# A convolution and two gated MLPs on one core: the head reordered, block 0's softmax first and block 1's moved to GpSimd

## The chip, the cores and the metric

The kernel runs on one core of a Trainium2 chip. Its time is the device time of one execution in microseconds; the median of the runs counts. The engines are TensorE (PE; its weight loads are shown as PEld), VectorE (DVE), ScalarE (ACT), GpSimd (POOL) and SyncE (SP), which only issues DMAs. A TensorE matmul writes PSUM; GpSimd reaches SBUF alone.

## The reference, cut to what matters

```python
# 2 x 4096 tokens of 192 features; 8 heads of 24 features, 7 taps
w = exp(weight_gen - max(weight_gen)); w = w / (sum(w) + 1e-9)      # over the 7 taps of a head
out[s, h] = sum_k w[s, h, k] * x_pad[s + k, h]                      # causal, 6 zero rows ahead
xn = out / sqrt(mean(out**2) + 1e-6) * rms_g
y = (silu(xn @ w_gate) * (xn @ w_val)) @ w_out                      # 192 -> 1536 -> 192
h = y @ w_in; z = (h * sigmoid(1.702 * h)) @ w_out2                 # 192 -> 2048 -> 192
```

All in float32. A matmul of the MLPs is made of three products of float32 halves (high by high, low by high, high by low), so each operand exists as a high and a low tile.

## The kernel before

The 8192 tokens lie on 128 partitions, 64 to each, and are worked off in 16 blocks of 4 columns (512 tokens). For a block, `conv_ops` makes the seven products with the softmax weights, their sum, the mean square (`sq`, ScalarE), its power -0.5 (`root`, GpSimd) and the scaled rows `xr`. `transpose_x` turns these to the four operands `xh`, `xl`, `xsh`, `xsl` (two transposed halves on TensorE; high part on ScalarE, low part on VectorE).

A *unit* is one step of the MLPs: `(1, b, m)` is block b's m-th of 12 up steps of the first MLP, `(2, b, i)` one of 8 of the second. `U1` issues its matmuls: 9 pairs (upper and lower half of the array run side by side) into `pg` and `pv`, then ScalarE's `silu` of `pg`; `second()` is VectorE's `p = p * pv` and ScalarE's copy `h`; `third()` is VectorE's `l = p - h`. `D1` is the unit's down product, 5 pairs, which go in with the matmuls of a later unit: `pend` holds them until unit i + 2. The list `units` is the order. Blocks 0 and 1 are interleaved, with block 0 `LAG` ahead: (1,0,0) (1,0,1) (1,1,0) (1,0,2) (1,1,1) (1,0,3) ... Before and after, unit 24 is (2,0,0), the first of the second MLP.

The engines work in the order in which the program issues (a manual schedule), so the place of a line in the main loop is its place in a queue.

The weights come as 64-bit words and are decoded *piece* by piece (`piece`), with three pieces in flight. A piece is `x1` on ScalarE, `x2`, `x2m` (masks) on VectorE; then `x3` (shift), `x4`, `x5` (low half) on VectorE; then `x6` (high half) on ScalarE. `x5` also loads the next piece by SP. `piece_steps` finishes the oldest piece in flight (`x6`), does `x3` to `x5` of the next and `x1` to `x2m` of the one behind it. `need` lists the pieces by the unit that first uses them, `run_work` forces them `LOOK` units ahead, and `some` spends each unit's credit (`room`), which is about one call of `piece_steps` in a unit.

The head stands ahead of the loop. Both blocks' softmaxes are made on VectorE (`softmax_ops`: maximum, subtraction, ScalarE's exponential, sum, 1e-9, reciprocal, product); block 0's weights lie in PSUM. Block 0's taps are VectorE's (14 products and 12 additions in PSUM), block 1's products GpSimd's, with TensorE summing them by a matmul with the identity (`ident`). Then squares and roots of both blocks, block 0's scaling and turn, and block 1's turn in unit 0.

The softmax of blocks 2 to 4 is started at unit `start_at`, that of (1, 1, 7); its exponential, between two table loads on ScalarE, stands one unit later. `Y` makes the second MLP's operands `yh`, `yl`, `ysh`, `ysl`.

Of the kernel before, what the change touches and what calls it, by code (L numbers as in the profile page):

```python
# [9 lines left out]
F32 = mybir.dt.float32  # L10
# [8 lines left out]
P = 128  # L19
# [11 lines left out]
BLOCKS = [4] * 16  # L31
GROUPS = [(0, 1), (1, 2), (2, 5), (5, 8), (8, 11), (11, 14), (14, 16)]
AHEAD = 4
LAG = 1
LAG2 = 3
NST = 3
LOOK = 1
# [5 lines left out]
def gated_conv_mlp(ctx: ExitStack, tc: tile.TileContext, xp, wg, w1, wo1, w2, wo2, g, out):  # L43
# [117 lines left out]
        nc.sync.dma_start(out=t, in_=wg[:, T0[b0] * 56:(T0[b0] + n) * 56])  # L161
        return t

    def softmax_ops(gi, t, dst=None):
# [5 lines left out]
        d = t if dst is None else dst  # L170
        d3 = d.rearrange("p (q k) -> p q k", k=TAPS)
        mx = smw.tile([P, G], F32, tag="mx", name=f"mx{gi}")
        step = 64
        parts = [(a, min(a + step, G)) for a in range(0, G, step)]
        pre, post = [], []
        for a, b in parts:
            def f(a=a, b=b):
                nc.vector.tensor_reduce(out=mx[:, a:b], in_=t3[:, a:b, :], axis=AX.X, op=ALU.max)

            def f2(a=a, b=b):  # L180
                nc.vector.tensor_tensor(
                    out=t3[:, a:b, :], in0=t3[:, a:b, :],
                    in1=mx[:, a:b].unsqueeze(2).to_broadcast([P, b - a, TAPS]), op=ALU.subtract)
            w = 7.5 * (b - a) + 70
            pre += [(w, f), (w, f2)]

        def ex():
            nc.scalar.activation(out=t, in_=t, func=AF.Exp)
        for a, b in parts:
            def f(a=a, b=b):  # L190
                nc.vector.tensor_reduce(out=mx[:, a:b], in_=t3[:, a:b, :], axis=AX.X, op=ALU.add)

            def f1(a=a, b=b):
                nc.vector.tensor_scalar_add(out=mx[:, a:b], in0=mx[:, a:b], scalar1=1e-9)
                nc.vector.reciprocal(out=mx[:, a:b], in_=mx[:, a:b])  # L195

            def f2(a=a, b=b):
                nc.vector.tensor_tensor(
                    out=d3[:, a:b, :], in0=t3[:, a:b, :],
                    in1=mx[:, a:b].unsqueeze(2).to_broadcast([P, b - a, TAPS]), op=ALU.mult)  # L200
            w = 7.5 * (b - a) + 70
            post += [(w, f), (4 * (b - a) + 150, f1), (w, f2)]
        for b in range(b0, b1):
            o = (T0[b] - T0[b0]) * 56
            wn_of[b] = d[:, o:o + BLOCKS[b] * 56].rearrange("p (q k) -> p q k", k=TAPS)
        return pre, ex, post

    def load_x(*bs):
        T = sum(BLOCKS[b] for b in bs)
        t0 = T0[bs[0]]  # L210
        t = big.tile([P, (T + HALO) * D], F32, tag="x", name=f"x{bs[0]}")
        cuts = [0] + [T0[b] + BLOCKS[b] + HALO - t0 for b in bs]
        for c0, c1 in zip(cuts, cuts[1:]):
            nc.sync.dma_start(out=t[:, c0 * D:c1 * D], in_=xp[:, (t0 + c0) * D:(t0 + c1) * D])
        for b in bs:
            xch[b] = t[:, (T0[b] - t0) * D:]

    def conv_ops(b):

# [14 lines left out]
        if b < 2:  # L234
            S = T // 2
            sums_of = [pacc.tile([P, NM], F32, tag=f"{n}{b}", name=f"{n}c_{b}") for n in "ab"]
            acc_of = [sums_of[j // S][:, (j % S) * D:(j % S + 1) * D] for j in range(T)]
        else:
            acc = att.tile([P, T, D], F32, tag="acc", name=f"acc{b}")
            acc_of = [acc[:, j] for j in range(T)]  # L240
        if b == 1:
            def tap(k):
                for i, ps in enumerate(sums_of):
                    tag = (("yh", "yl"), ("ysh", "ysl"), ("yh0", "yl0"))[k % 3][i]
                    pr = ytp.tile([P, NM], F32R, tag=tag, name=f"pr{k}_{i}").bitcast(F32)[:, :S * D]
                    mul(nc.gpsimd, k, pr, i * S, (i + 1) * S)
                    nc.tensor.matmul(ps[:, :S * D], ident, pr, start=k == 0, stop=k == TAPS - 1)
            ops += [(cost, lambda k=k: tap(k)) for k in range(TAPS)]
        elif b == 0:
            n = S * D  # L250

            def tap(k):
                for i, ps in enumerate(sums_of):
                    mul(nc.vector, k, prod[:, i * n:(i + 1) * n] if k else ps[:, :n], i * S, (i + 1) * S)
                for i, ps in enumerate(sums_of if k else ()):
                    nc.vector.tensor_tensor(out=ps[:, :n], in0=ps[:, :n], in1=prod[:, i * n:(i + 1) * n], op=ALU.add)  # L256
            ops += [(cost, lambda k=k: tap(k)) for k in range(TAPS)]
        else:
            total = acc.rearrange("p t d -> p (t d)")

# [9 lines left out]
        def sq():  # L270
            room = xr if b != 1 else ytp.tile([P, NM], F32R, tag="yh", name="sq1").bitcast(F32).unsqueeze(1)
            for j in range(T):
                nc.scalar.activation(out=room[:, j if b != 1 else 0, 0:D], in_=acc_of[j], func=AF.Square,
                                     accum_out=ss[:, j:j + 1])
        ops.append((1500, sq))

        def root():
            nc.gpsimd.tensor_scalar(out=ss, in0=ss, scalar1=1.0 / D, scalar2=1e-6,
                                    op0=ALU.mult, op1=ALU.add)
            nc.gpsimd.tensor_tensor(out=ri, in0=ss, in1=half[:, :T], op=ALU.pow)  # L280
        ops.append((500, root))

        def sc(j):
            nc.vector.tensor_scalar_mul(out=xr[:, j, 0:D], in0=acc_of[j], scalar1=ri[:, j:j + 1])
            if b >= TURN:
                return
            i = (j + T // 2) % T if b < 2 else j
            nc.scalar.mul(out=xr[:, i, D:2 * P], in_=acc_of[i][:, P:D], mul=ri[:, i:i + 1])
        for j in range(T):
            ops.append((230, lambda j=j: sc(j)))  # L290
        xrow[b] = xr
# [36 lines left out]
    def transpose_x(b, halves=False):  # L328
# [6 lines left out]
        l = xtp.tile([P, NM], F32R, tag="xl", name=f"xl{b}")  # L335
        sh = xtp.tile([P, NM], F32R, tag="xsh", name=f"xsh{b}")
        sl = xtp.tile([P, NM], F32R, tag="xsl", name=f"xsl{b}")
        pa, pb = sums(b, "x_")
        xT[b] = (h, l, sh, sl)
        if halves:  # L340

# [13 lines left out]
        def split(acts=True, dves=True):  # L355
            for c, ps, i in parts:
                h_, l_ = ((h, l), (sh, sl))[c]
                h_, l_ = h_[:, :N], l_[:, :N]
                if i is not None:
# [239 lines left out]

    units = []  # L600
    for m in range(M1):
        units += [(1, 0, t) for t in range(len([u for u in units if u[1] == 0]), min(M1, m + LAG + m // 3 + 1))]
        units += [(1, 1, m)]
    for t in range(PAIRS + LAG2):
        units += [(2, 0, t)] if t < PAIRS else []
# [111 lines left out]
    with ExitStack() as order:  # L717
# [11 lines left out]
        warm = sml.tile([P, TM], F32, tag="ri", name="warm")  # L729
        nc.scalar.activation(out=warm, in_=half, func=AF.Exp)  # L730
        wn0 = pu.tile([P, NM], F32, tag="u", name="wn0")
        pre, ex, post = softmax_ops(0, sm[0], wn0[:, 0:BLOCKS[0] * 56])
        pre1, ex1, post1 = softmax_ops(1, sm[1])
        run(pre)
# [1 line left out]
        run(pre1)  # L736
        ex1()
        run(post)
        run(post1)
        nc.scalar.activation(out=warm, in_=half, func=AF.Silu)  # L740
        conv, conv1 = conv_ops(0), conv_ops(1)
        run(conv[:TAPS])
        run(conv1[:TAPS])
        for r in line:
            r[0].pop(0)()
        for f in [c[TAPS + k][1] for c in (conv, conv1) for k in range(2)]:
            f()
        for f in line[0].pop(0) + line[0].pop(0) + line[1].pop(0):
            f()
        for f in line.popleft().pop(0):  # L750
            f()
        run(conv[TAPS + 2:])
        split = transpose_x(0)
        for f in line[0].pop(0):
            f()
        split()
        for f in line[0].pop(0):
            f()
        line[0].append([])
        run(conv1[TAPS + 2:])  # L760
# [8 lines left out]
        for i, u in enumerate(units):  # L769
# [67 lines left out]
            second, third = (U1 if kind == 1 else U2)(b, m, lambda *ups: matmuls(ups, downs, kind == 2 and b < 2))  # L837
            todo = [v / 2 for v in (room(i) if i < pos[1, 2, 0] else (share(0, i), share(1, i)))]
            if i == 0:
                split = transpose_x(1)  # L840
                split(dves=False)
                second()
                split(acts=False)
                third()
                some(todo)
                some(todo)
                for f in line[0].pop(0):
                    f()
            elif i < pos[1, 2, 0]:
                run(behind)  # L850
# [73 lines left out]
```

## Time and profile before

| | |
|---|---|
| runs | 1229.76 us median of 3 (1228.94 to 1229.93) |
| profiled execution | 1228.96 us |
| its span, first to last instruction | 1227.0 us |
| granted TensorE clock, mean | 0.998 |

The profile is of one execution. Times are microseconds from the span's start. An engine is busy while it executes an instruction; what it waits for stands in brackets behind the first instruction after the pause. Where short instructions overlap, the distance between two starts is what one costs its engine, and the duration what the next engine waits for. The granted clock is a share of 2.4 GHz.

### The profile page before, as it was taken

The numbers are of one execution on the slowest core, as the hardware profiler recorded it, in microseconds if no ns is written. First come the engines' busy times: TensorE is split into PE (matmuls) and PEld (weight loads), VectorE is DVE, ScalarE is ACT, GpSimd is POOL, SyncE is SP. The second block draws the span as 40 slices with busy tenths as digits, with TensorE's granted clock in tenths as the row PEclk, the third lists the DMA queues.
The fourth block names the chain that finished last, engine by engine and source line by source line (L and its number), as shares of the span: only waits on it lengthen the run. The fifth ranks groups of instructions, "written<-read, shape, count | busy, mean of one in ns | idle before, by whom it ended". The sixth has DMA issues, their size and how long they took to land.

```text
span 1227.0 us, 26917 instructions
## 1 busy us (share of the span) xinstructions
PE 1210.3 (99%) x10316; PEld 1114.1 (91%) x10316; DVE 774.3 (63%) x1300; ACT 651.0 (53%) x1275; POOL 32.1 (3%) x53
## 2 busy tenths in 40 slices
PE   6999999999999999999999999999999999999998
PEld 3888999988999999999999998999988888988897
DVE  8998967857465574755747567464665746545432
ACT  4667664644545455464545645445464544544553
POOL 4000000000000000000000000000000000000000
PEclk9999999999999999999999999999999999999999
DMA  6884311010111001100100011010110011000000
GB/s 203 255 253 148 116 57 47 1 41 24 33 43 34 13 20 34 30 33 17 60 6 26 34 31 34 10 31 33 31 33 13 20 34 31 1 16 17 1 14 13
DMA packets 35615, 58.03 MB, mean 47 GB/s; under 512 B 8288, under 2 KB 21344, under 8 KB 35488
## 3 DMA queue, kind: packets, MB, share of 16 engines
q1 hardware_dynamic: 35264, 56.13, 14.7%
q8 instruction: 81, 1.33, 0.5%
q14 instruction: 46, 0.38, 0.1%
q10 hardware_dynamic: 224, 0.20, 0.1%
HBM read 43.71 MB, written 6.29 MB: 41 GB/s over the span
## 4 chain that ended last, share of the span: by engine, by line
PE 96%; DVE 2%; ACT 1%; issue 0%; DMA 0%; POOL 0%; DVEq 0%; POOLq 0%; ACTq 0%
PE a L381 24%; PE ph L381 22%; PE pg L381 18%; PE b L381 17%; PE pv L381 15%; DVE xr L229 0%; DVE p L490 0%; DVE ac L256 0%; DVE bc L256 0%; DMA wraw<-in_wg 0%; PE ax L352 0%; POOL ri L280 0%; DVE l L494 0%; ACT h L491 0%; DVE mx L195 0%
## 5 line engine op out<-in xcount | busy, mean ns | idle before, releaser
L381 PE MATMUL a<-h,o 64*128 64x512 f32 x1788 | 517.4, 391 | 0.0
L381 PEld LDWEIGHTS a<-h,o 64*128 64x128 f32 x1788 | 328.5, 184 | 13.7
L514 DVE TENSOR_TENSOR l<-p,h 128x512 fp32r<-128x512 f32 x256 | 176.1, 691 | 242.5 <-ACT p L508 241.1
L381 PE MATMUL b<-h,o 64*128 64x512 f32 x896 | 310.8, 392 | 0.0
L381 PE MATMUL b<-l,o 64*128 64x512 f32 x896 | 310.4, 392 | 0.0
L381 PE MATMUL a<-l,o 64*128 64x512 f32 x894 | 309.3, 391 | 0.0
L507 ACT ACTIVATE h<-ph 128x512 fp32r<-128x512 f32 x256 | 153.7, 600 | 204.2 <-PE ph L381 198.2
L381 PE MATMUL pv<-xh,w 64*128 64x512 f32 x768 | 240.8, 393 | 0.2
L381 PE MATMUL pg<-xh,w 64*128 64x512 f32 x768 | 239.8, 391 | 0.0
L381 PE MATMUL ph<-yh,w 64*128 64x512 f32 x1024 | 235.4, 392 | 0.1
L491 ACT CAST h<-p 128x512 fp32r<-128x512 f32 x192 | 119.3, 621 | 177.4 <-DVE p L490 177.3
L486 ACT ACTIVATE p<-pg 128x512 f32<-128x512 f32 x192 | 114.6, 597 | 166.4 <-PE pg L381 150.6
L490 DVE TENSOR_TENSOR p<-p,pv 128x512 f32<-128x512 f32 x192 | 131.6, 685 | 98.4 <-PE a L381 68.2
L494 DVE TENSOR_TENSOR l<-p,h 128x512 fp32r<-128x512 f32 x192 | 132.6, 691 | 77.0 <-ACT h L491 77.0
L381 PEld LDWEIGHTS b<-l,o 64*128 64x128 f32 x896 | 165.7, 185 | 8.5 <-DVE l L494 0.3
L381 PEld LDWEIGHTS a<-l,o 64*128 64x128 f32 x894 | 165.1, 185 | 7.7
L381 PEld LDWEIGHTS b<-h,o 64*128 64x128 f32 x896 | 164.4, 185 | 6.8 <-POOLq L396 0.3
L381 PEld LDWEIGHTS ph<-yh,w 64*128 64x128 f32 x1024 | 146.3, 185 | 11.7 <-ACT yh L543 0.5
L508 ACT ACTIVATE p<-ph 128x512 f32<-128x512 f32 x256 | 153.6, 600 | 0.0
L381 PE MATMUL ph<-yl,w 64*128 64x512 f32 x512 | 152.4, 392 | 0.1
L381 PE MATMUL pv<-xl,w 64*128 64x512 f32 x384 | 150.4, 392 | 0.0
L381 PE MATMUL pg<-xl,w 64*128 64x512 f32 x384 | 150.2, 391 | 0.0
(117 smaller groups left out, 2092.5 us busy)
## 6 DMA issues: line engine op xcount, KB each, us to landing
x<-in_xp SPq DMA_DIRECT2D x15, 960.0 KB, 4.7
st<-in_w SPq DMA_DIRECT2D x20, 384.0 KB, 4.2
zt<-in_w SPq DMA_DIRECT2D x20, 384.0 KB, 3.6
st<-in_wo SPq DMA_DIRECT2D x14, 384.0 KB, 4.1
zt<-in_wo SPq DMA_DIRECT2D x14, 384.0 KB, 3.5
out_z<-za SPq DMA_DIRECT2D x15, 256.0 KB, 2.2
xl<-raw SPq DMA_DIRECT2D x192, 16.0 KB, 1.8
xsl<-raw SPq DMA_DIRECT2D x192, 16.0 KB, 1.8
```

Of the source, the lines that this page charges most:

```text
L381: ins = nc.tensor.matmul(ps[:, :N], w[rows], x[rows, :N], start=start, stop=stop)
L486: nc.scalar.activation(out=p[:, :N], in_=pg[:, :N], func=AF.Silu)
L490: nc.vector.tensor_tensor(out=p[:, :N], in0=p[:, :N], in1=pv[:, :N], op=ALU.mult)
L491: nc.scalar.copy(h[:, :N], p[:, :N])
L494: nc.vector.tensor_tensor(out=l[:, :N], in0=p[:, :N], in1=h[:, :N].bitcast(F32), op=ALU.subtract)
L507: nc.scalar.activation(out=h[:, :N], in_=ps[j][:, :N], func=AF.Silu, scale=SIG)
L508: nc.scalar.activation(out=p[:, :N], in_=ps[j][:, :N], func=AF.Silu, scale=SIG)
L514: nc.vector.tensor_tensor(out=l[:, :N], in0=p[:, :N], in1=h[:, :N].bitcast(F32), op=ALU.subtract)
```

## The change

- Block 1's softmax: its sum is five small GpSimd operations (`by_gpsimd`), its reciprocal stays on VectorE, between block 0's first two products (`between`), and its product is GpSimd's.
- Block 0's and block 1's columns of `x` come in three DMAs instead of two; the first has five columns.
- Block 0: TensorE sums taps 0 and 1 by matmuls with the identity; VectorE adds the others. The last tap's sums are written to SBUF (`tot3`), with a 193rd column whose square is the 1e-6, so that `root` needs only the power.
- Block 1: ScalarE makes tap 6 in 32 products of 24 columns, GpSimd the other six taps.
- Matmuls of the identity: ten at the start, two of `x` behind the taps.
- The order behind the taps is written out anew; block 1's squares stand ahead of block 0's scaling on ScalarE. Block 0 is turned through other PSUM buffers. Block 1 is turned behind unit 1, no longer behind unit 0, and its scaling is two operations on VectorE.
- Units: `FIRST` gives (1,0,0) (1,0,1) (1,1,0) (1,1,1) (1,0,2) (1,1,2) (1,0,3) (1,0,4) (1,1,3) ... The down products of units 0 and 1 both go into unit 3. The first pieces are issued at other places, and (1, 1, 7) is unit 17 instead of 18.
- In units of the second MLP, up to block 2, what is due late is issued between the two halves of the credit.

```diff
-LAG = 1
+FIRST = (2, 2, 3, 5, 6, 7, 9, 10) + (M1,) * 4
...
+        def by_gpsimd():
+            three = hid.tile([P, NM], F32, tag="p", name="three")
+            v = three[:, :G * 3].rearrange("p (q k) -> p q k", k=3)
+            def plus(out, x, y):
+                nc.gpsimd.tensor_tensor(out=out, in0=x, in1=y, op=ALU.add)
+            plus(v, t3[:, :, 0:3], t3[:, :, 3:6])
+            total = mx.unsqueeze(2)
+            plus(total, v[:, :, 0:1], v[:, :, 1:2])
+            plus(total, total, v[:, :, 2:3])
+            plus(total, total, t3[:, :, 6:7])
+            nc.gpsimd.tensor_scalar_add(out=mx, in0=mx, scalar1=1e-9)
+            def rest():
+                nc.vector.reciprocal(out=mx, in_=mx)
+                nc.gpsimd.tensor_tensor(out=t3, in0=t3, in1=total.to_broadcast([P, G, TAPS]), op=ALU.mult)
+            return rest
-        return pre, ex, post
+        return pre, ex, by_gpsimd if gi == 1 else post
...
-        cuts = [0] + [T0[b] + BLOCKS[b] + HALO - t0 for b in bs]
+        cuts = [0] + [BLOCKS[0] + 1] * (t0 == 0) + [T0[b] + BLOCKS[b] + HALO - t0 for b in bs]
...
+                    if k < TAPS - 1:
+                        mul(nc.gpsimd, k, pr, i * S, (i + 1) * S)
+                    else:
+                        for q in range(S * HEADS):
+                            c = (k + i * S) * D + q * GRP
+                            nc.scalar.mul(out=pr[:, q * GRP:(q + 1) * GRP], in_=x[:, c:c + GRP],
+                                          mul=wn[:, i * S * HEADS + q, k:k + 1])
+                        for r in list(line)[i:2 * i + 1]:
+                            r[0].pop(0)()
+                    nc.tensor.matmul(ps[:, :S * D], ident, pr, start=k == 0, stop=k == TAPS - 2)
+            ops += [(cost, lambda k=k: tap(k)) for k in (0, 1, 2, 3, 4, 6, 5)]
...
+            def taps():
+                for k in range(TAPS - 1):
+                    product(k, 0)
+                    if k == 0:
+                        between.pop()()
+                    product(k, 1)
+                    if k < 2:
+                        both(add, k)
+                    elif k > 2:
+                        both(add, k - 1)
+                nc.vector.memset(tot3[:, :, D:D + 1], (1e-6 * D) ** 0.5)
+                for i in range(2):
+                    product(TAPS - 1, i)
+                    add(TAPS - 2, i)
+                    add(TAPS - 1, i)
...
-        pa, pb = sums(b, "x_")
+        pa, pb = sums(b, "x_") if b else [pu.tile([P, NM], F32, tag="u", name=f"{n}x_0") for n in "ab"]
...
+        heat = pu.tile([P, NM], F32, tag="u", name="heat")
+        for _ in range(10):
+            nc.tensor.matmul(heat[:, :P], ident, ident, start=True, stop=True)
...
+        run(taps0)
+        run(taps1)
+        for _ in range(2):
+            nc.tensor.matmul(heat[:, :2 * D], ident, xch[0][:, 0:2 * D], start=True, stop=True)
+        sq0()
+        root0()
+        (a1, a2), (a3, a4, a5), a6 = line.popleft()
+        for f in [a1, a2, a3] + a6 + [a4, a5]:
+            f()
+        sq1()
+        scale0()
+        root1()
+        split = transpose_x(0)
+        (b1, b2), (b3, b4, b5), b6 = line.popleft()
+        b1()
+        b2()
+        split(only=(0,))
+        b3()
+        split(only=(1,))
+        for f in b6 + [b4, b5]:
+            f()
+        scale1()
         sm[2] = softmax_load(2)
-        for p, _ in need[1:]:
-            add_work(0, max(0, p - LOOK), [(1780, piece_steps)])
+        for k, (p, _) in enumerate(need[2:]):
+            add_work(0, p - LOOK if k > 1 else 3 + k, [(1780, piece_steps)])
...
             if i == 0:
+                second()
+                (c1, c2), (c3, c4, c5), c6 = line[0]
+                c1()
+                c2()
+                third()
+            elif i == 1:
                 split = transpose_x(1)
                 split(dves=False)
                 second()
                 split(acts=False)
+                for f in [c3] + c6 + [c4]:
+                    f()
                 third()
-                some(todo)
-                some(todo)
-                for f in line[0].pop(0):
+                c5()
+                line[0].clear()
+                for f in line[1].pop(0):
                     f()
...
                 some(todo)
+                if kind == 2:
+                    while late:
+                        late.pop(0)()
                 some(todo)
...
-                pend.append((i + 2, D1, (b, m)))
+                pend.append((max(i + 2, 3), D1, (b, m)))
```

## Rows read from the trace of the kernel before

**Rows 1.** The page's engine lines: busy us, share of the span, instructions.

```profile
PE 1210.3 (99%) x10316; PEld 1114.1 (91%) x10316; DVE 774.3 (63%) x1300; ACT 651.0 (53%) x1275; POOL 32.1 (3%) x53
```

**Rows 2.** Stretches: busy us (instructions) per engine, granted clock, DMA share, GB/s.

```profile
0.00:10.00 10.00, 1.88 (x3) 1.16 (x4) 6.85 (x19) 4.31 (x7) 3.53 (x11) 1.00 0.81 289
...
20.10:23.40 3.30, 0.00 (x0) 0.00 (x0) 2.85 (x9) 3.04 (x15) 2.83 (x4) 1.00 0.75 171
23.80:27.10 3.30, 3.30 (x17) 2.50 (x17) 3.06 (x7) 2.19 (x5) 0.00 (x0) 0.50 0.70 208
```

**Rows 3.** The chain that ended last, in the head: start, us, what.

```profile
19.19 1.05 ACT xr L273 x6
...
23.42 0.84 PE ax L352 x4
```

**Rows 4.** TensorE's timeline: start us, us, engine, line, operation, out<-in, count.

```profile
25.04 0.79 PE L381 MATMUL pg<-xh,w 64*128 64x512 f32 x1
...
28.75 0.66 PE L352 MATMUL ax<-ident,xr 128*128 128x128 f32 x4
...
32.35 0.39 PE L381 MATMUL pg<-xh,w 64*128 64x512 f32 x1
...
38.98 0.39 PE L381 MATMUL pg<-xh,w 64*128 64x512 f32 x1
...
48.74 0.39 PE L381 MATMUL pg<-xh,w 64*128 64x512 f32 x1
```

**Rows 5.** TensorE's weight loads ahead of the second MLP: pause and releaser.

```profile
104.57 0.30 PEld L381 LDWEIGHTS ph<-yh,w 64*128 64x128 f32 x4 [0.55 <-ACT yh L543]
105.42 0.19 PEld L381 LDWEIGHTS ph<-yl,w 64*128 64x128 f32 x2 [0.55 <-DVE yl L546]
```

**Rows 6.** VectorE's timeline in the head.

```profile
5.34 0.40 DVE L198 TENSOR_TENSOR wn<-wraw,mx 128x224 f32<-128x224 f32 x1
...
6.98 0.56 DVE L229 TENSOR_TENSOR ac<-x,wn 128x384 f32<-128x384 f32 x1
...
18.59 0.56 DVE L256 TENSOR_TENSOR bc<-bc,xr 128x384 f32<-128x384 f32 x1
19.05 0.36 DVE L99 TENSOR_SCALAR dec_s<-st 128x384 int32<-128x384 int32 x1
...
19.58 0.58 DVE L107 SCALAR_TENSOR_TENSOR dec_a<-dec_a,dec_s 128x384 int32<-128x384 int32 x1
...
25.02 0.75 DVE L364 SCALAR_TENSOR_TENSOR xl<-ax,gt,xh 128x512 fp32r<-128x512 f32 x1
```

**Rows 7.** The two DMAs of `x` in the head: us from issue to landing.

```profile
DMA to landing us min/median/max: 5.3/5.6/5.8
```

**Rows 8.** GpSimd's timeline in the head.

```profile
7.21 11.52 POOL L229 TENSOR_TENSOR pr<-x,wraw 128x384 f32<-128x384 f32 x14 [5.87 <-DVE wraw L198]
...
20.69 1.35 POOL L280 TENSOR_TENSOR ri<-ss,half 128x4 f32<-128x4 f32 x1
22.12 0.19 POOL L278 TENSOR_SCALAR ss<-ss 128x4 f32<-128x4 f32 x1
```

**Rows 9.** ScalarE's timeline in the head.

```profile
4.44 0.39 ACT L188 ACTIVATE wraw<-wraw 128x224 f32<-128x224 f32 x1 [0.33 <-DVE wraw L181]
...
20.11 0.34 ACT L273 ACTIVATE sq<-ac 128x192 f32<-128x192 f32 x1
...
21.48 0.33 ACT L273 ACTIVATE sq<-bc 128x192 f32<-128x192 f32 x1
...
22.20 0.52 ACT L288 ACTIVATE xr<-bc,ri 128x64 f32<-128x64 f32 x2
...
24.30 0.69 ACT L362 ACTIVATE xh<-ax,gt 128x512 fp32r<-128x512 f32 x1 [0.93 <-PE ax L352]
```

**Rows 10.** VectorE and ScalarE behind the unit that begins at 48.74.

```profile
52.34 0.69 DVE L490 TENSOR_TENSOR p<-p,pv 128x512 f32<-128x512 f32 x1 [0.20 <-ACT p L486]
...
53.59 0.51 ACT L122 CAST w<-dec_a 128x384 fp32r<-128x384 f32 x1
```

More of the change, by code (lines that the diff above doesn't have):

```diff
@@ L162, in softmax_load, with softmax_ops @@
         return t
-    def softmax_ops(gi, t, dst=None):
+    def softmax_ops(gi, t, first=None):
         b0, b1 = GROUPS[gi]
@@ L169, in softmax_ops @@
         t3 = t.rearrange("p (q k) -> p q k", k=TAPS)
-        d = t if dst is None else dst
-        d3 = d.rearrange("p (q k) -> p q k", k=TAPS)
         mx = smw.tile([P, G], F32, tag="mx", name=f"mx{gi}")
@@ L198, in f2 @@
                 nc.vector.tensor_tensor(
-                    out=d3[:, a:b, :], in0=t3[:, a:b, :],
-                    in1=mx[:, a:b].unsqueeze(2).to_broadcast([P, b - a, TAPS]), op=ALU.mult)
+                    out=(t if first is None else first).rearrange("p (q k) -> p q k", k=TAPS)[:, a:b, :],
+                    in0=t3[:, a:b, :], in1=mx[:, a:b].unsqueeze(2).to_broadcast([P, b - a, TAPS]), op=ALU.mult)
             w = 7.5 * (b - a) + 70
@@ L204, in softmax_ops @@
             o = (T0[b] - T0[b0]) * 56
+            d = t if first is None else first
             wn_of[b] = d[:, o:o + BLOCKS[b] * 56].rearrange("p (q k) -> p q k", k=TAPS)
-        return pre, ex, post
+        def by_gpsimd():
[14 more added lines that the diff above has]
+        return pre, ex, by_gpsimd if gi == 1 else post
     def load_x(*bs):
@@ L216, in load_x @@
             xch[b] = t[:, (T0[b] - t0) * D:]
+    between = []
     def conv_ops(b):
@@ L238, in conv_ops @@
         else:
-            acc = att.tile([P, T, D], F32, tag="acc", name=f"acc{b}")
+            acc = att.tile([P, T * (D + 1)], F32, tag="acc", name=f"acc{b}")[:, :T * D].rearrange("p (t d) -> p t d", d=D)
             acc_of = [acc[:, j] for j in range(T)]
@@ L243, in tap @@
                 for i, ps in enumerate(sums_of):
-                    tag = (("yh", "yl"), ("ysh", "ysl"), ("yh0", "yl0"))[k % 3][i]
+                    tag = (("yh", "yl"), ("ysh", "ysl"), ("yh0", "yl0"))[2 if k == TAPS - 1 else k % 2][i]
                     pr = ytp.tile([P, NM], F32R, tag=tag, name=f"pr{k}_{i}").bitcast(F32)[:, :S * D]
-                    mul(nc.gpsimd, k, pr, i * S, (i + 1) * S)
-                    nc.tensor.matmul(ps[:, :S * D], ident, pr, start=k == 0, stop=k == TAPS - 1)
@@ L248, in conv_ops @@
-            ops += [(cost, lambda k=k: tap(k)) for k in range(TAPS)]
+                    if k < TAPS - 1:
[7 more added lines that the diff above has]
+                            r[0].pop(0)()
@@ L249, in conv_ops @@
+                    nc.tensor.matmul(ps[:, :S * D], ident, pr, start=k == 0, stop=k == TAPS - 2)
+            ops += [(cost, lambda k=k: tap(k)) for k in (0, 1, 2, 3, 4, 6, 5)]
         elif b == 0:
             n = S * D
[L252 to L256, printed above, removed]
@@ L257, in conv_ops, with place, product @@
-            ops += [(cost, lambda k=k: tap(k)) for k in range(TAPS)]
+            tot = att.tile([P, T * (D + 1)], F32, tag="acc", name="spare")
+            zs = [zp.tile([P, NM], F32, tag=tag, name=f"{tag}c") for tag in ("za", "zb")]
+            def place(k, i):
+                return zs[i][:, :n] if k % 3 == 2 else (prod, tot)[k % 3][:, i * n:(i + 1) * n]
+            tot3 = tot.rearrange("p (t d) -> p t d", d=D + 1)
+            acc_of = [tot3[:, j, 0:D] for j in range(T)]
+            def product(k, i):
+                mul(nc.vector, k, place(k, i), i * S, (i + 1) * S)
@@ new lines, in add @@
+            def add(k, i):
+                ps, of = sums_of[i][:, :n], place(k, i)
+                if k < 2:
+                    nc.tensor.matmul(ps, ident, of, start=k == 0, stop=k == 1)
+                elif k < TAPS - 1:
+                    nc.vector.tensor_tensor(out=ps, in0=ps, in1=of, op=ALU.add)
+                else:
+                    nc.vector.tensor_tensor(
+                        out=tot3[:, i * S:(i + 1) * S, 0:D], in0=ps.rearrange("p (t d) -> p t d", d=D),
+                        in1=of.rearrange("p (t d) -> p t d", d=D), op=ALU.add)
@@ new lines, in both @@
+            def both(f, k):
+                f(k, 0)
+                f(k, 1)
+            def taps():
[4 more added lines that the diff above has]
+                    product(k, 1)
+                    if k < 2:
+                        both(add, k)
[6 more added lines that the diff above has]
+                    add(TAPS - 1, i)
@@ L258, in conv_ops @@
+            ops.append((cost, taps))
         else:
@@ L268, in conv_ops, with sq @@
         ri = sml.tile([P, T], F32, tag="ri", name=f"ri{b}")
[L270 to L275, printed above, removed]
+        def sq(j0=0, j1=T):
+            for j in range(j0, j1):
+                if b == 0:
+                    junk = hid.tile([P, NM], F32, tag="p", name=f"sq0_{j}")
+                    nc.scalar.activation(out=junk[:, 0:D + 1], in_=tot3[:, j], func=AF.Square, scale=D ** -0.5,
+                                         accum_out=ss[:, j:j + 1])
+                    continue
+                if b == 1:
+                    room = ytp.tile([P, NM], F32R, tag="yh", name=f"sq{j}").bitcast(F32)[:, 0:D]
+                else:
+                    room = xr[:, j, 0:D]
+                nc.scalar.activation(out=room, in_=acc_of[j], func=AF.Square, accum_out=ss[:, j:j + 1])
@@ L277, in root, with scale @@
         def root():
-            nc.gpsimd.tensor_scalar(out=ss, in0=ss, scalar1=1.0 / D, scalar2=1e-6,
-                                    op0=ALU.mult, op1=ALU.add)
+            if b:
+                nc.gpsimd.tensor_scalar(out=ss, in0=ss, scalar1=1.0 / D, scalar2=1e-6,
+                                        op0=ALU.mult, op1=ALU.add)
             nc.gpsimd.tensor_tensor(out=ri, in0=ss, in1=half[:, :T], op=ALU.pow)
-        ops.append((500, root))
+        xrow[b] = xr
+        if b < 2:
+            def scale():
+                for j in range(T if b == 0 else 0):
+                    nc.vector.tensor_scalar_mul(out=xr[:, j, 0:D], in0=acc_of[j], scalar1=ri[:, j:j + 1])
+                    nc.scalar.mul(out=xr[:, j, D:2 * P], in_=acc_of[j][:, P:D], mul=ri[:, j:j + 1])
+                if b == 0:
+                    return
+                for j in range(T):
+                    nc.scalar.mul(out=xr[:, j, D:2 * P], in_=acc_of[j][:, P:D], mul=ri[:, j:j + 1])
+                for i in range(2):
+                    rows = slice(i * S, (i + 1) * S)
+                    nc.vector.tensor_tensor(
+                        out=xr[:, rows, 0:D], in0=sums_of[i][:, :S * D].rearrange("p (t d) -> p t d", d=D),
+                        in1=ri[:, rows].unsqueeze(2).to_broadcast([P, S, D]), op=ALU.mult)
+            return ops, sq, root, scale
@@ L283, in sc @@
+        ops += [(1500, sq), (500, root)]
         def sc(j):
             nc.vector.tensor_scalar_mul(out=xr[:, j, 0:D], in0=acc_of[j], scalar1=ri[:, j:j + 1])
[L285 to L288, printed above, removed]
+            if b < TURN:
+                nc.scalar.mul(out=xr[:, j, D:2 * P], in_=acc_of[j][:, P:D], mul=ri[:, j:j + 1])
         for j in range(T):
@@ L290, in conv_ops @@
             ops.append((230, lambda j=j: sc(j)))
-        xrow[b] = xr
         return ops
@@ L353, in transpose_x, with split @@
             parts = [(c, ps[:, :N], None) for c, ps in enumerate((pa, pb))]
-        def split(acts=True, dves=True):
+        def split(acts=True, dves=True, only=(0, 1)):
             for c, ps, i in parts:
+                if c not in only:
+                    continue
                 h_, l_ = ((h, l), (sh, sl))[c]
@@ L601, in gated_conv_mlp @@
     for m in range(M1):
-        units += [(1, 0, t) for t in range(len([u for u in units if u[1] == 0]), min(M1, m + LAG + m // 3 + 1))]
+        units += [(1, 0, t) for t in range(len([u for u in units if u[1] == 0]), FIRST[m])]
         units += [(1, 1, m)]
@@ L738, in gated_conv_mlp @@
         run(post)
-        run(post1)
+        between.append(post1())
         nc.scalar.activation(out=warm, in_=half, func=AF.Silu)
[L741 to L746, printed above, removed]
-            f()
-        for f in line[0].pop(0) + line[0].pop(0) + line[1].pop(0):
-            f()
[L750 to L753, printed above, removed]
-        for f in line[0].pop(0):
[L755 to L760, printed above, removed]
+        (taps0, sq0, root0, scale0), (taps1, sq1, root1, scale1) = conv_ops(0), conv_ops(1)
+        run(taps0)
[6 more added lines that the diff above has]
+        for f in [a1, a2, a3] + a6 + [a4, a5]:
+            f()
+        sq1()
[9 more added lines that the diff above has]
+        for f in b6 + [b4, b5]:
+            f()
+        scale1()
         sm[2] = softmax_load(2)
-        for p, _ in need[1:]:
-            add_work(0, max(0, p - LOOK), [(1780, piece_steps)])
+        for k, (p, _) in enumerate(need[2:]):
+            add_work(0, p - LOOK if k > 1 else 3 + k, [(1780, piece_steps)])
         nxt = 2
@@ L843, in gated_conv_mlp @@
                 split(acts=False)
+                for f in [c3] + c6 + [c4]:
+                    f()
                 third()
-                some(todo)
-                some(todo)
-                for f in line[0].pop(0):
+                c5()
+                line[0].clear()
+                for f in line[1].pop(0):
                     f()
```

## The prediction

> **What bounds the kernel now.** I read the engine lines of the page first: TensorE is busy 99% of the span [rows 1], so a change moves the end only through time in which TensorE cannot work. Then the stretches of the head: no matmul between 20.1 and 23.4 us, and in the next stretch, to 27.1, the granted clock is 0.50, the 1.2 GHz level [rows 2]. Then the chain of waits, which says what the idle head is for: VectorE's seven taps of block 0, ScalarE's squares at 19.19, GpSimd's power, the scaling, the transposes at 23.42 [rows 3]. Last TensorE's own timeline: the first product is at 25.04, the fifth unit starts at 38.98, and three units later it is 48.74 [rows 4]. That is 3.25 us a unit of 14 pairs of matmuls, 0.232 a pair, without a pause. The one later wait that I find is for the second stage's first operands, 0.55 us for `yh` and 0.55 for `yl` [rows 5].
>
> The measure is therefore the start of the fifth unit. In both orders four units' up products and two units' down products stand before it, so the same matmuls.
>
> **The taps of block 0.** Before, the first product is at 6.98 and the 26th operation at 18.59, 0.464 apart, done at 19.15 [rows 6]. After, block 0's weights are ready at 5.34 + 0.40, so its first product starts at about 5.8 instead. Its data comes in an earlier, half as large transfer: now all 960 KB land 5.3 us after an issue at 1.63, at 6.93 [rows 7], and the 480 KB that no longer precede the landing take 1.7 us at the stretch's 289 GB/s [rows 2], so 5.2; in time. At nothing, then; were the half as late as the whole, 1.2 us.
>
> The new wait is the reciprocal for block 1 between the first two products: VectorE stands until GpSimd has five small sums, and 23 operations of block 0 are queued behind it. The sums start when block 1's exponential ends, 4.44 + 0.39, plus 0.09. The trace has no small addition on GpSimd. Lower bound: a 4-element multiply-add, 0.19. Upper bound: the 4-element power, 1.35 [rows 8]. The 384-element product takes 11.52 / 14 = 0.823 us, 2.1 ns an element, so from 0.19 up I take 0.36 for the 96 elements, 0.25 for each of three of 32, 0.2 for the last, and 0.08 between them: 1.65, so 6.55. Reciprocal at 6.6, next product at 6.9. Then 23 operations at 0.464 (10.7), 0.1 for a memset, 0.26 for two additions that now directly follow the one they depend on, 0.1 for the tail: 18.1. Gain 1.05; by the lower bound 1.4, by the upper a loss of 3.3.
>
> During that chain VectorE's multiply at 5.34, 0.40 long, has both inputs in SBUF [rows 6]; no row shows such an instruction beside a GpSimd one. The Trainium skill (SBUF — State Buffer, the section on the two separate sides) says the two then take a shared port in turns, the later one waiting for the whole of the earlier. By that the chain ends up to 0.4 later and the time is 0.4 more; by the rows alone it is not.
>
> Hidden: GpSimd's twelve products end at 7.65 + 12 x 0.823 = 17.5, under VectorE; each us beyond 18.9 would hold the power back by one. ScalarE's 32 products of 24 columns have no row; two of 64 columns take 0.52 [rows 9], so at most 0.26 x 32 = 8.3, and a gain is excluded, since they are new work. Begun at 7.95 with three decodings between they end by 17.8 at worst, before the squares' last half at 18.1; whatever runs over that delays the squares one for one. The twelve matmuls on the identity run while TensorE has nothing else. The third part of `x` puts every later transfer of SP's queue one issue back; the first of them is decoded only behind ScalarE's 16 products, so it isn't late.
>
> **From the taps to the first product.** Before 25.04 - 19.15 = 5.9. After, the squares read SBUF and the power needs no preparing step: squares done 18.9, power 1.35 on, 20.3. But that isn't what ends last. ScalarE's queue is: the copy of the first weights' high half waits for two masks and a shift on VectorE (18.0 + 0.53 + 0.57 [rows 6]) and ends at 19.5, then four squares of block 1 at 0.46 each (20.11 to 21.48 [rows 9]), 21.35, then four scalings, 0.85 (two take 0.52), 22.2, then `xh`, 0.69. First product at 22.9: 2.1 us earlier, half of it from the taps and half from here.
>
> **The clock.** TensorE's gap shrinks from 3.3 us without a matmul to about 1.1, then scattered transposes. I take the 2.4 GHz level. If it falls all the same, unit 0 takes up to the 3.71 of before (25.04 to 28.75 [rows 4]) instead of 3.1: 0.6 later, or 1.3 if unit 1 is slow too.
>
> **Units 0 to 3.** Unit 0: its sixth pair waits for VectorE's second split, two of 0.7 and a shift after 22.9 [rows 6], 24.8, and three pairs and a hand-over follow: 26.05. A unit without down products and block 1's transposes took 28.75 to 32.35, 3.6 [rows 4]: 29.6. Before, another unit lay between the transposes and their first user. Now the user is next, and waits for ScalarE's unit-1 activation and `xh`: 30.0. Unit 2 without down products is 2.6 long, 2.7 with a late split: 32.7. Unit 3 has both held-back down products, 19 pairs, 4.4: 37.1. So far 1.85 ahead of 38.98.
>
> **The fifth unit's weights.** It is (1, 0, 2), and needs the high half of piece `w1_2`. Before, that copy was pulled forward to the end of unit 0's instructions. Now its steps are: first list in unit 1, decoding in unit 2's `piece_steps`, and the high half in unit 3's, which is issued behind `second()`. On ScalarE it stands behind unit 3's activation and `h`, and so waits for unit 3's own products. A unit begun at 48.74 has its `p` at 52.34 and the next high-half copy at 53.59, done 54.10: 5.36 from its start [rows 10]. In a unit of 19 pairs `pv` ends three pairs later: 6.06. TensorE is done after 4.4, so it waits 1.65 to 1.7: the fifth unit starts at 38.85. Gain left: 0.1.
>
> **Later.** Unit 5's start forces a second piece into one unit, so VectorE is late and unit 7 waits for another high half: 0.3 (0 to 0.5). Against that, the exponential of blocks 2 to 4 moves one unit ahead of the second stage, so part of the wait for `yh` and `yl` goes: 0.5 (0 to 0.9, nearly all of [rows 5]). The splits of the second stage's first units are issued earlier between pieces: nothing, TensorE has no other wait there.
>
> Sum: -0.1 + 0.3 - 0.5 = -0.3. The profiled execution took 1228.96 us (span 1227.0), 0.8 below the median of the runs; both move alike, 1229.76 - 0.3 = 1229.4. A measurement of this kernel tells about 0.2%, 2.46 us, from no change.
>
> **Rivals.** (A) The forecast, 1229.4: 0.56.
>
> (B) The high half isn't late, because ScalarE or the semaphores let it pass earlier than the row of unit 48.74 says. Then 1.7 more is kept, 1227.7, and with all of the later wait gone 1227.3. For it: TensorE never waited for such a half before. Against it: program order. 0.20.
>
> (C) The clock stays at the lower level in units 0 and 1, or in the first sums: 1230.0 to 1230.7. For it: it fell after a gap of 3.3 us; against: the new gap is a third of that. 0.15.
>
> (D) The slower side: GpSimd's small sums cost what its 4-element power does. Four at 1.35 with 0.08 between end at 10.8, all of block 0 stands 4.3 behind, 1233.7. The forecast turns slower when the reciprocal waits until 9.5, that is from a mean of 0.83 for each of five sums. For it: the only other few-element GpSimd row is dear; against: the 4-element multiply-add next to it takes 0.19. 0.09.
>
> **Numbers.** Faster by over 0.2% (below 1227.3): half of B and 0.02 of A, 0.12. Slower (above 1232.2): D and little else, 0.10. Within: 0.78. The range leaves out B's better half and D: 1227.2 to 1231.9.
>
> **What the new profile would show.** Right: first product near 22.9, block 0's last tap near 18.1, a reciprocal on VectorE that waits for GpSimd near 6.3, and TensorE waiting about 1.7 us at its fifth unit for ScalarE's copy into `w1_2`. Wrong: that unit starting without a wait (B), matmul pairs 0.42 apart after 23 us (C), the reciprocal later than 9 (D). I'd also be wrong if a wait that I haven't listed held TensorE for more than 2 us between 40 and 110 us, where the order of the units is new.

## The result, and the profile after

The changed kernel takes **1236.88 us** (median of 4 runs, 1236.73 to 1237.31) against 1229.61 in the runs beside it: ratio 1.0059, 95% interval 1.0046 to 1.0072. It is slower by 7.3 us, three times the 2.46 us that count as a difference here.

The head first. TensorE's timeline of the changed kernel, which answers to [rows 4]:

```profile
23.70 0.49 PE L464 MATMUL pg<-xh,w 64*128 64x512 f32 x1 [0.24 <-ACT xh L445]
...
29.74 0.66 PE L433 MATMUL ax<-ident,xr 128*128 128x128 f32 x4
...
31.17 0.49 PE L464 MATMUL pg<-xh,w 64*128 64x512 f32 x1 [0.34 <-ACT xh L445]
...
38.36 0.39 PE L464 MATMUL b<-l,o 64*128 64x512 f32 x1
39.80 0.49 PE L464 MATMUL pg<-xh,w 64*128 64x512 f32 x1 [1.04 <-ACT w L122]
```

The first product is at 23.70, before at 25.04. The fifth unit is at 39.80, before at 38.98; it could have followed the pair of 38.36 by 0.23 us and waits 1.2 us for ScalarE's copy into `w`. ScalarE's timeline shows that copy behind the fourth unit's `h`, done at 39.75:

```profile
22.98 0.67 ACT L445 ACTIVATE xh<-ax,gt 128x512 fp32r<-128x512 f32 x1
...
38.71 0.62 ACT L574 CAST h<-p 128x512 fp32r<-128x512 f32 x1 [1.21 <-DVE p L573]
39.24 0.51 ACT L122 CAST w<-dec_a 128x384 fp32r<-128x384 f32 x1
```

GpSimd's small sums, which no row of before had, and its products and power [rows 8]:

```profile
5.34 0.37 POOL L210 TENSOR_TENSOR three<-wraw 128x96 f32<-128x96 f32 x1 [4.00 <-ACT wraw L186]
5.79 0.47 POOL L210 TENSOR_TENSOR mx<-three 128x32 f32<-128x32 f32 x1
6.34 0.26 POOL L210 TENSOR_TENSOR mx<-mx,three 128x32 f32<-128x32 f32 x1
6.68 0.27 POOL L210 TENSOR_TENSOR mx<-mx,wraw 128x32 f32<-128x32 f32 x1
7.03 0.30 POOL L216 TENSOR_SCALAR mx<-mx 128x32 f32<-128x32 f32 x1
...
8.46 9.89 POOL L247 TENSOR_TENSOR pr<-x,wraw 128x384 f32<-128x384 f32 x12
19.74 1.04 POOL L348 TENSOR_TENSOR ri<-ss,half 128x4 f32<-128x4 f32 x1 [1.39 <-ACT sq L335]
```

VectorE's timeline [rows 6], with its wait for block 1's weights, the reciprocal's wait and the last tap:

```profile
4.02 0.39 DVE L176 TENSOR_REDUCE mx<-wraw 128x32 f32<-128x224 f32 x1 [0.43 <-DMA wraw<-in_wg]
...
5.77 0.40 DVE L196 TENSOR_TENSOR wn<-wraw,mx 128x224 f32<-128x224 f32 x1
...
7.37 0.35 DVE L219 RECIPROCAL mx<-mx 128x32 f32<-128x32 f32 x1 [0.61 <-POOL mx L216]
...
18.21 0.56 DVE L295 TENSOR_TENSOR spare<-bc,xr 128x384 f32<-128x384 f32 x1
```

So TensorE is 0.8 us late at the fifth unit, not 7. Where is the rest? The page's engine lines [rows 1] have TensorE busy for 1225.5 us instead of 1210.3, with about the same number of matmuls:

```profile
PE 1225.5 (99%) x10348; PEld 1177.1 (95%) x10348; DVE 772.2 (63%) x1294; ACT 658.2 (53%) x1307; POOL 32.1 (3%) x56
```

That is no wait. The chart below compares the start of the n-th activation of `pg` or `ph` on ScalarE (from the timelines of both kernels): it follows TensorE, and no record of it is missing.

```
n (from 0)                12      60      100     200     447 (last)
before, us                68.0    192.5   307.0   563.8   1218.8
after minus before, us    +1.2    +1.8    +2.7    +4.5    +8.5
```

A wait would make one step. This grows all the way, some 0.65 us for each 100 us. The profile of each kernel is of one execution. Between 300 and 1150 us TensorE never pauses in either kernel; the changed one's waits of its weight loads in this stretch are

```profile
PEld b L464 <- POOLq L479: 0.3, 2, 0.2
```

(in total, times, longest). Still fewer matmuls go through. The stretches view of the kernel before, 300 to 1150 us (columns as in [rows 2]: stretch, length, then busy us and instructions of TensorE, its weight loads, VectorE, ScalarE and GpSimd, clock, DMA share, GB/s):

```profile
300.00:1150.00 850.00, 850.00 (x7310) 793.42 (x7308) 504.15 (x779) 432.46 (x823) 13.21 (x22) 1.00 0.09 26
```

and of the changed kernel:

```profile
300.00:1150.00 850.00, 850.00 (x7263) 827.05 (x7261) 502.38 (x776) 431.55 (x821) 13.22 (x22) 1.00 0.09 26
```

A pair of matmuls (upper and lower rows) takes 850 / (7310 / 2) = 0.2326 us before and 0.2341 after, 0.65% more at a granted clock of 1.00. This **pair step** is read in the same way in every run below. In the groups of instructions of this stretch all kinds of products are slower alike, the mean of one 393 or 394 ns where before shows 390 to 392; before and after:

```profile
L381 PE MATMUL a<-h,o 64*128 64x512 f32 x1270 | 368.0, 391 | 0.0
...
L381 PE MATMUL pg<-xh,w 64*128 64x512 f32 x564 | 175.3, 390 | 0.0
```

```profile
L464 PE MATMUL a<-h,o 64*128 64x512 f32 x1264 | 368.0, 393 | 0.0
...
L464 PE MATMUL pg<-xh,w 64*128 64x512 f32 x560 | 175.6, 393 | 0.0
...
L464 PE MATMUL ph<-yh,w 64*128 64x512 f32 x704 | 162.2, 393 | 0.0
```

The instructions there are the same. What differs is where their operands lie. `acc` and `spare` grew from 768 to 772 floats, which the program rounds up to 32 bytes more, and every SBUF tile allocated behind them (`xh` to `xsl`, `yh` to `ysl`, `h`, `l`) moved by 32 bytes; the weights, allocated ahead, did not (six of their tiles trade places, multiples of 256 bytes apart). The excerpt of the diff above leaves that growth out; the whole diff has it. In the list of addresses of the built program, block 5's `xh` goes from 147776 to 147808, and the first weight tile stays at 17088. The three new tiles in PSUM also turn the banks: `pg`, `pv` use 2,0 and 3,1 before, 1,2 and 3,0 after.

### The profile page after: what moved, and what is told of

The parts are those of the page before. It is cut to its first block, busy times and chain, and to the rows that moved or that the text cites. A ratio compares the mean times of both kernels' runs of the same rounds, so it can differ in the third digit from the quotient of the medians.

```text
span 1235.4 us, 27006 instructions
## 1 busy us (share of the span) xinstructions
PE 1225.5 (99%) x10348; PEld 1177.1 (95%) x10348; DVE 772.2 (63%) x1294; ACT 658.2 (53%) x1307; POOL 32.1 (3%) x56
## 4 chain that ended last, share of the span: by engine, by line
PE 97%; DVE 2%; ACT 0%; issue 0%; DMA 0%; POOL 0%; SPq 0%; DVEq 0%; POOLq 0%
PE a L464 25%; PE ph L464 22%; PE b L464 17%; PE pg L464 17%; PE pv L464 16%; DMA wraw<-in_wg 0%; DVE p L573 0%; DVE ac L293 0%; DVE dec_a L107 0%; DVE bc L293 0%; DVE spare L247 0%; DVE xr L247 0%; DVE xl L447 0%; DVE xsl L447 0%; ACT sq L342 0%
## 5 line engine op out<-in xcount | busy, mean ns | idle before, releaser
L464 PEld LDWEIGHTS a<-h,o 64*128 64x128 f32 x1788 | 324.1, 185 | 5.1
L464 PE MATMUL ph<-yh,w 64*128 64x512 f32 x1024 | 239.2, 393 | 0.0
L464 PEld LDWEIGHTS ph<-yh,w 64*128 64x128 f32 x1024 | 150.7, 185 | 7.1
L464 PE MATMUL ph<-yl,w 64*128 64x512 f32 x512 | 155.9, 394 | 0.0
```

The costliest lines, as they stand in the source:

```text
L464: ins = nc.tensor.matmul(ps[:, :N], w[rows], x[rows, :N], start=start, stop=stop)
```

## The experiments

Weight slices start multiples of 256 bytes apart, and so do the moving operands (the tiles that TensorE streams past the loaded weights) among themselves, but for runs 7 and 10. One number therefore tells the placement: how far the moving operand starts behind its weights, modulo 256 bytes. For all 10240 matmuls of 512 columns it is 128 before (147776 - 17088 is 510 x 256 + 128), and 160 after. "Gap" below is a tile that nothing uses. The other tiles behind `acc`, such as `p` and `yt`, which VectorE and ScalarE read and write, move along with `x`'s and `y`'s operands in every run.

**1. The changed kernel, put back to a multiple of 64 (distance 192).**

```diff
-acc = att.tile([P, T * (D + 1)], ...)[:, :T * D]...
+acc = att.tile([P, T * D + 16], ...)[:, :T * D]...
-tot = att.tile([P, T * (D + 1)], F32, tag="acc", name="spare")
+tot = att.tile([P, T * D + 16], ...)[:, :T * (D + 1)]
```

> The changed kernel with one edit: the tile acc/spare is 784 floats long (3136 bytes) instead of 772 (3088), so that every SBUF tile behind it starts at a multiple of 64 bytes again, as in the kernel before, and not 32 bytes off one. Nothing else moves. Theory A (the start of TensorE's moving operands in SBUF sets its pace): the mean step from pair to pair between 300 and 1150 us falls from 234.2 ns to the 232.7 ns of before, and of the 8.5 us by which the last matmul starts late some 6.5 go: 1230.0 to 1231.0. Theory B (the pairs of PSUM banks of pg and pv, which the change turned from 2,0 and 3,1 to 1,2 and 3,0, set it): 1236.9, as the change. Theory C (the changed head's order and waits carry on through the run): 1236.9.

Measured: 1232.89 us, ratio to before 1.0026 (1.0015 to 1.0037), pair step 233.3 ns. More than half of the loss goes with 32 bytes more of padding, less than theory A said: 64 bytes is not the whole rule.

**2. The kernel before, moved by 32 bytes (distance 160).**

```diff
-acc = att.tile([P, T, D], F32, tag="acc", ...)
+acc = att.tile([P, T * (D + 1)], ...)[:, :T * D].rearrange(...)
```

> The kernel before with one edit: acc is allocated with 772 floats (768 of them used), so that every SBUF tile behind it starts 32 bytes further; no instruction is added, removed or moved. Theory A (alignment): the pair step rises to 234.2 ns and the time to 1235.5 to 1236.5. Theories B (banks) and C (the head's order): 1229.6.

Measured: 1237.10 us, 1.0062 (1.0049 to 1.0076). The instructions are those of the kernel before, in the same order, and it has the whole loss. Its stretch:

```profile
300.00:1150.00 850.00, 850.00 (x7262) 817.07 (x7260) 501.96 (x776) 430.50 (x821) 13.19 (x22) 1.00 0.09 26
```

**3. The kernel before with the changed kernel's banks (distance 128).**

```diff
+none0 = pu.tile([P, NM], F32, tag="u", name="none0")
+nc.tensor.matmul(none0[:, :P], ident, ident, start=True, stop=True)
 wn0 = pu.tile([P, NM], F32, tag="u", name="wn0")
```

> The kernel before with one matmul of 128 columns into one more PSUM tile ahead of the head, so that pg and pv get the banks 0,3 and 1,2 instead of 2,0 and 3,1: the pairing of the changed kernel. SBUF stays as before. Theory A (alignment): 1229.6 within 1 us. Theory B (banks): 1235.5 to 1237. Theory C (the head's order): 1229.6.

Measured: 1229.93 us, 1.0002 (0.9993 to 1.0010), step 232.7. The changed pairing of banks costs nothing: theory B is out.

**4. Experiment 1 with the fifth unit's high half early (distance 192).**

```diff
 run_work(i)
+if i == 3:
+    for f in line[0].pop(0):
+        f()
```

> The kernel of e1_aligned with the high half of the fifth unit's weights (ScalarE's copy of w1_2) made ahead of unit 3's activation instead of behind its p and h. In the changed kernel that copy starts at 39.24 us and TensorE waits 1.4 us for it (38.36 to 39.80). If that stall is real time: the fifth unit starts at 38.4, and the kernel takes 1.2 to 1.6 us less than e1_aligned, so by theory A 1228.5 to 1229.8, by B and C 1235.5. If something else holds the fifth unit or the time comes back later (yh at unit 24): no less than 0.5 us below e1_aligned.

Measured: 1231.66 us, 1.0015 (1.0006 to 1.0024), 1.2 below experiment 1. ScalarE now copies at 36.26, ahead of the activation,

```profile
36.26 0.50 ACT L122 CAST w<-dec_a 128x384 fp32r<-128x384 f32 x1
36.67 0.59 ACT L569 ACTIVATE p<-pg 128x512 f32<-128x512 f32 x1
```

and the fifth unit follows the fourth without a pause, at 38.03 instead of experiment 1's 39.27:

```profile
37.86 0.39 PE L464 MATMUL b<-l,o 64*128 64x512 f32 x1
38.03 0.40 PE L464 MATMUL pg<-xh,w 64*128 64x512 f32 x1
```

The stall is real time; the n-th activations stay 1.5 to 1.7 us ahead of experiment 1's to the end.

**5. The same, moved on to 128 bytes (distance 0).** `T * D + 32` instead of `T * D + 16`.

> The kernel of e4_aligned_early_high with acc/spare 800 floats long, so that the SBUF tiles behind it stand 128 bytes further than in the kernel before, instead of 64. So far the mean pair step between 300 and 1150 us is 232.6 ns at a shift of 0, 234.2 at 32 and 233.4 at 64. Theory A1 (the pace goes by the start modulo 128 bytes): the step is 232.6 ns again, and the kernel 3.5 us below e4: 1228.0 to 1228.6, faster than the kernel before. Theory A2 (anything off the old addresses costs, or only the 32 bytes do and e4's rest has another cause): the step stays at 233.3 and the time at 1231.7. Theory C (the changed order, not the address, makes the 233.4): 1231.7.

Measured: **1202.90 us, 0.9790** (0.9776 to 0.9805), step 227.6. The direction of A1, and eight times its size: the kernel before was itself at a slow place.

**6. The kernel before, weights and all moved by 32 bytes (distance 128).**

```diff
+gap = const.tile([P, 8], F32, name="gap")
+nc.gpsimd.memset(gap, 0.0)
 ident = const.tile([P, P], F32, name="ident")
```

> The kernel before with 32 bytes (8 floats, cleared once by GpSimd) ahead of everything in SBUF: weights, x and all later tiles move together by 32 bytes, so that the distance of TensorE's moving operands from its weights stays. Theory A-absolute (the start of the moving operands as such): 234.2 ns a pair and 1236 to 1237, as e2. Theory A-relative (the distance between weights and moving operands): 232.6 ns and 1229.9.

Measured: 1229.21 us, 1.0003 (0.9994 to 1.0012), step 232.5. `xh` is at 147808 here as in experiment 2, without its loss. The address as such is out; the distance from the weights counts.

**7. The kernel before, `h` and `l` of blocks 2 to 15 moved by 32 bytes (x and y 128, h and l 160).** As in 6, with the gap ahead of the last pools, which also hold the decoding's buffers and a tile `raw`.

> The kernel before with 32 bytes ahead of the tiles h and l of blocks 2 to 15 alone; xh, xl, yh, yl and the weights stay. If each matmul pays for the start of its own moving operand: the products from h and l into a and b rise to 234.2 ns, those from x and y into pg, pv and ph stay at 232.6, and the time is 1229.9 + 0.43 x 6.2 = 1232 to 1233. If it is the distance between operands that are read at the same time, both kinds may rise: 1233 to 1237. If h and l don't matter: 1229.9.

Measured: 1228.46 us, 0.9996 (0.9987 to 1.0006), step 232.3. No loss at all; the simple reading "each matmul pays for its own operand" fails.

**8. The kernel before, moved by 64 bytes (distance 192).** As 2, with `T * D + 16`.

> The kernel before with acc 784 floats long, all tiles behind it 64 bytes further, no instruction changed. Theories A1 and A2 in which the address alone counts: 233.4 ns a pair, as e1, and 1229.9 + 0.0033 x 1150 = 1233 to 1234. Theory C (e1's 233.4 came from the changed order of the head): 232.6 ns and 1229.9.

Measured: 1233.08 us, 1.0037 (1.0023 to 1.0050), step 233.3, as experiment 1.

**9. The kernel before, 128 bytes behind the weights (distance 0).**

```diff
+gap = ctx.enter_context(tc.tile_pool(name="gap", bufs=1)).tile([P, 32], F32, name="gap")
+nc.gpsimd.memset(gap, 0.0)
 big = ctx.enter_context(tc.tile_pool(name="big", bufs=1))
```

> The kernel before with a gap of 128 bytes (32 floats, cleared once by GpSimd) right behind the weights in SBUF: x, the softmax weights, xr, acc and all tiles behind them move by 128 bytes against the weights, and keep their distances from one another. Theory W (the pace goes by the distance between the weights and the moving operands; at 128 more both start at the same place modulo 256): 227.2 ns a pair, and 1229 - 5.4/232.6 x 1180 = 1202. Theory X (the distance of the moving operands from x, xr and acc, which VectorE and GpSimd read at the same time): 232.6 ns and 1229. Against e5 at the same pace it also prices the change with the early high half: by the prediction's sum e5 is 0.3 to 2 us below this kernel.

Measured: 1204.26 us, 0.9792 (0.9778 to 0.9807). Theory W: `x`, `xr` and `acc` moved along, so their distances from the moving operands are those of before. The stretch, at a step of 227.5 ns:

```profile
300.00:1150.00 850.00, 850.00 (x7474) 837.25 (x7472) 509.20 (x787) 443.00 (x846) 13.20 (x22) 1.00 0.09 26
```

**10. As 9, with the tiles of 7 another 128 bytes on (x and y 0, h and l 128).**

> As e9_before_gap128, and a second gap of 128 bytes ahead of the tiles h and l of blocks 2 to 15: x and y stand 128 bytes off their old distance from the weights, h and l 256. If each product pays for its own operands and 256 counts as 0: the products into a and b step at 232.6 ns, those into pg, pv and ph at 227.2, and the time is 1202 + 0.44 x 27 = 1214. If a period of 256 is wrong and any multiple of 128 will do: 1202. If the worst operand sets the pace of all: 1229.

Measured: 1220.50 us, 0.9923 (0.9907 to 0.9940), step 231.1:

```profile
300.00:1150.00 850.00, 850.00 (x7356) 840.86 (x7355) 506.26 (x782) 437.66 (x831) 13.19 (x22) 1.00 0.09 26
```

That is 70% of the way from 227.5 back to 232.6, where products that pay for their own operands alone would give 44%. So the place of `h` and `l` matters too, but not through their own products alone: in the trace, where a pair that reads `x` or `y` follows another such pair, their starts lie 231.7 ns apart on average (228.1 in run 9), and where a pair that reads `h` or `l` follows another, 231.1 (227.3 in run 9). Products that read at distance 0 are as slow here as those that read at 128. Why they are isn't shown, and neither is it shown that TensorE's reading of `h` and `l` costs the time, and not ScalarE's and VectorE's writing of them.

**11. As 9, with 256 bytes (distance 128 again).**

> As e9_before_gap128 with a gap of 256 bytes. If the distance counts modulo 256: 232.6 ns a pair and 1229, as before. If it counts modulo 512 or more, or any further distance helps: another pace, by e9's side 1202.

Measured: 1230.11 us, 1.0000 (0.9990 to 1.0009), step 232.7. 256 bytes further is the pace of before, 128 further (run 9) is not: so far as these runs go, the pace repeats after 256 bytes.

**12. As 9, with 96 bytes (distance 224).**

> As e9_before_gap128 with a gap of 96 bytes, 32 short of the fast one. If only the very place is fast (starts equal modulo 256): 233 to 234.5 ns a pair and 1231 to 1237. If the pace falls smoothly towards it: 229 to 230 ns and 1211 to 1217. If 96 is as good as 128: 1202.

Measured: 1232.81 us, 1.0024 (1.0015 to 1.0034), step 233.2. The fast place is narrow on this side: 32 bytes short of it, nothing is left. Distances from 32 to 96 were not run.

The runs by distance (ns of a pair; ratio to before):

```
distance   pair step                       ratio of times
0          227.5 (9), 227.6 (5)            0.9792, 0.9790 (5 with the early half)
128        232.6 (before), 232.5 to 232.7  1.0000 to 1.0003 (3, 6, 11)
160        234.1 (after), 234.1 (2)        1.0059, 1.0062
192        233.3 (1), 233.3 (8), 233.2 (4) 1.0026, 1.0037, 1.0015 (4 with the early half)
224        233.2 (12)                      1.0024
```

## Why the prediction was wrong

**The step that failed** is the one behind the timeline: "0.232 a pair, without a pause", and from it "the measure is therefore the start of the fifth unit". It took the pair step as a constant that the change can't touch, and summed waits alone: the step's own change stood in the sum at nothing, without a reason. The step went to 0.2341; over the 1190 us from the first products to the last that is 0.0015 / 0.2326 x 1190 = 7.7 us, and experiment 2 has 7.2 of it without any of the change. No rival covers it, and neither does the list of what would make the forecast wrong, which looks for one long wait between 40 and 110 us. The change did hold it: a tile that grows by four floats ahead of the moving operands.

**The sum itself.** Against the kernel before at the same distance, the change does nothing that can be measured: 1.0059 beside 1.0062 at 160, 1.0026 beside 1.0037 at 192; at 0, with the early half, 0.9790 beside 0.9792. The -0.3 us lies within that, but its sign is not settled: the profiled executions have the changed kernel later, not earlier. In the traces at 160 the n-th activation is 1.1 us later in the changed kernel at n = 12, 1.0 at 60, 100 and 0.8 at the end; it doesn't grow, so what the head and the order of the units cost is paid early, and nothing is added later. At 192 (experiment 1 against 8) it is 0.4 at n = 12 and at the end.

**Its terms.** *The small sums* end at 7.33, 1.99 us after they begin, where 1.65 was worked out; 32 elements cost 0.26 and 0.27, as estimated. The 0.47 of the second one stands beside VectorE's multiply of 5.77, with both inputs in SBUF, and is 0.48 beside the same multiply in experiments 1, 4 and 5. The port taken in turns, of which the Trainium skill speaks (SBUF — State Buffer, the section on the two separate sides), would explain the 0.2 over its neighbours, half of the 0.4 that the prediction gave as the most; no run here separates it. *Block 1's weights* landed late: VectorE waits for them to 4.02, where experiment 1's execution, without that wait, does the same at 3.50, and those of experiments 4 and 5, with the same head, at 3.53 and 3.57: this half microsecond is chance of one execution. Both together put the reciprocal at 7.37 for 6.6, the last tap's end at 18.77 for 18.1, the first product at 23.70 for 22.9 (23.16 in experiment 1), and the fifth unit at 39.80 for 38.85 (39.27 in experiment 1). *GpSimd's products* end at 18.35 and ScalarE's 32 products, 6.8 us in all, at 15.55, hidden as said.

**The stall behind unit 3** is as forecast, in place, cause and order of size: 1.2 us for 1.65, since the unit's end moved too. Experiment 4 takes it away and gains 1.2 us, so of the rivals (B) describes what could be had, not what happened. (C) didn't come: the granted clock stays at 1.00, the 2.4 GHz level,

```profile
20.00:30.00 10.00, 9.11 (x51) 5.52 (x50) 7.83 (x19) 6.83 (x23) 2.00 (x3) 1.00 0.66 190
```

and once the first pairs, 0.33 to 0.45 apart with a wait for `xl`, are through, the fourth and fifth (24.82 and 25.06) are 0.24 apart. (D) didn't either: the reciprocal is ahead of 9.5 by 2.1 us. *Later:* the second wait for a high half, at unit 7, came and was smaller than the 0.3 forecast: the unit starts at 49.86, 0.36 behind the last pair of unit 6, so 0.13 are lost.

```profile
49.86 0.18 PEld L464 LDWEIGHTS pg<-xh,w 64*128 64x128 f32 x1 [0.41 <-ACT w L122]
```

Between n = 16 and n = 20 the changed kernel regains 0.4 us at the second stage's first operands, 0.5 forecast, and gives 0.3 back near 124 us, at `yl` of the next block.

**What stays open.** Experiments 2, 6, 9 and 11 show that the distance between the weights and the tiles behind `acc`, the moving operands among them, sets the pace. What in the chip makes it so isn't shown. That TensorE's reads of weights and of moving operands meet somewhere in SBUF is argued from this alone; the tiles that VectorE and ScalarE read and write moved along in each of these runs, and experiment 10 doesn't fit a cost that each product pays for its own operand.

## What to carry to other kernels

Where TensorE is busy all the time, its step is a term of the sum: work out the ns of a pair from a stretch without pauses, before and after, ahead of any search for waits. A loss that grows evenly over the run is a pace, one that appears as a step is a wait. When a change alters the size of any SBUF tile, look at what moves behind it, and undo the move alone before judging the change; here a gap of 128 bytes, of no use to the program, is worth 26 us, more than the 16.7 us of the span in which TensorE wasn't busy before [rows 1].

## What was unexpected of the hardware

Matmuls of 64 rows and 512 columns, in pairs, with a weight load each, step at 227.5 ns when weights and moving operands start at the same place modulo 256 bytes, and at 232.5 to 234.1 ns at distances of 128 to 224: 2.2 to 2.9% more, with weight loads as long as ever (184 or 185 ns each, before, after and in experiment 9). A place 32 bytes short of the fast one cost all of it. The Trainium skill (SBUF — State Buffer, "Who interferes with whom") gives TensorE two independent reading ports, one for the moving operand and one for weight loads, and has only VectorE and GpSimd wait for one another. By that the placement would change nothing; experiments 2, 6 and 9 show that it does.
